# A recurrent-memory attention kernel: the order of loads, turns and value tails around its first segment

## The chip, the cores and the metric

The kernel runs on one core of a Trainium2 chip. The metric is device time in microseconds (us), the median of three runs; one further execution was profiled, and every line of a profile shown here is from such an execution. The engines are TensorE (PE, with its weight loads as PEld), VectorE (DVE), ScalarE (ACT), GpSimd (POOL) and SyncE (SP), which here does nothing but issue DMA transfers. DMA transfers are issued on SP's queue and on ACT's.

## What is computed

Two layers over 2048 tokens of width 640. The first is attention with a recurrent memory: the layer-normed tokens are cut into 64 segments of 32, each is put behind 8 memory rows, and the first 8 output rows of a segment are the memory of the next one. The second is a feed-forward layer with a squared ReLU. Cut to what matters:

```python
mem = mem0                                    # 8 x 640
for s in range(64):
    h = concatenate([mem, x[32 * s:32 * s + 32]])      # 40 x 640
    q, k, v = h @ Wq, h @ Wk, h @ Wv          # 32 heads of 128
    p = softmax(mask(q k^T * scale))          # memory columns open, the rest causal
    o = (p v) @ Wo                            # 40 x 640
    mem = o[:8]
    outs.append(o[8:])
h = x + concatenate(outs)
out = h + squared_relu(layernorm(h) @ w1 + b1) @ w2 + b2
```

The weights Wq, Wk, Wv and Wo are 5.24 MB each in bf16 and are kept on the core.

## The kernel before

**Segments, blocks and tails.** Four segments make a block of 128 tokens; there are 16 blocks (NB). One call of step(b, sp) (L459) works on segment sp of block b, and the recurrence makes the 64 steps a chain: the memory part of step s needs the output projection of step s - 1. A segment's 8 memory rows and first 24 tokens are the main rows, 32 in all, in tile hT4. The last 8 tokens of each segment, the tail, depend on no memory, so their q, k and v are projected a block at a time, away from the chain: load_tail_rows(g) (L144) loads the tails of four blocks (group g), ln_stats, ln_norm and ln_transpose (L184 to L229) turn them into hTt, and tail_units(b, which) (L312) gives ten pieces of work of four matmuls each, two halves of five. When a half is done, tail_out (L357) evacuates it on ACT: q and k are flipped into place by DVE, through the list late; v rows are stored to the DRAM tile vt_d and loaded back in another order by tails_v_in (L409) into vt4, one slot for each segment of the block.

**Row buffers and parking.** rowtile (L259) gives one of four buffers in turn for an evacuated row of 512. A value row goes instead into a place of the list parked, as long as there are any: memory that is used later for something else (hnT0, ht0, oTts, vt4s[1], hT4s[1], the v tile of step 1). It is then stored later, by the list stores, which the loop empties by 7, 5 and 5 at the starts of the steps (0, 1), (0, 2) and (0, 3). Before, there are 17 places, and block 0's rows don't use them: they are stored at once on ACT's queue.

**Fill.** The lists fill, late, mid, owed and soon hold work that steps take up at set places: run(q, n) does n pieces of q. What remains of fill is run at the end of a step, where PE would otherwise wait for the chain through mem_to_hT (L291).

**Before the first step.** Lines L155 to L160 and L825 to L837 issue the loads: x of block 0, the memory rows (four small loads on ACT's queue into a zeroed tile om, L156), tail group 0, Wv in five chunks, tail group 1, Wq, Wk, tail group 2, Wo in six pieces, x of block 1. All but the memory rows are on SP's queue. start() (L766) then projects segment 0 together with the tails of block 0 in three streams (v, q, k), chunk by chunk of the weights, into one PSUM tile pa; it puts tail units of later blocks between the chunks. Its result v0 makes step(0, 0) run with ready set: it has no projections of its own and takes fill in their place.

**Queues.** The order of the work is the program's (L109): each engine and each DMA queue does its instructions in the order in which the code issues them. PSUM has a pool mm of three buffers for single products and transposes, one buffer ch for scores and the output projection pw, and one of four banks for pa and po. wo_rounds (L273) does the output projection in 16 rounds; rounds 0 to 8 (the end left out, as in the calls) need the even heads of Wo, which are loaded first, rounds 8 to 12 the next two pieces, rounds 12 to 16 the last two.

Of the kernel before, what the change touches and what calls it, by code (L numbers as in the profile page):

```python
# [11 lines left out]
F32 = mybir.dt.float32  # L12
BF16 = mybir.dt.bfloat16
# [3 lines left out]
def kernel(  # L17
# [16 lines left out]
    nc = tc.nc  # L34
# [43 lines left out]
    ident = const.tile([128, 128], BF16)  # L78
    o_ring = [const.tile([64, DH], BF16, name="o%d" % k) for k in range(5)]
    o0 = const.tile([128, DC, 32], BF16, name="om")  # L80
    nc.vector.memset(o0[:], 0.0)
    make_identity(nc, ident[:])
# [47 lines left out]

    def load_w(w, src):
        w2d = src.rearrange("d h e -> d (h e)")
        for c in range(DC):
            nc.sync.dma_start(out=w[:, c * HE:(c + 1) * HE], in_=w2d[c * 128:(c + 1) * 128, :])
# [20 lines left out]
    load_x(0)  # L155
    for q in range(4):  # L156
        nc.scalar.dma_start(out=o0[32 * q:32 * q + M],  # L157
                            in_=A_mem0[0].rearrange("m (c q f) -> q m c f", q=4, f=32)[q])
    load_tail_rows(0)
    load_w(wv, A_Wv)  # L160

# [22 lines left out]
    def ln_stats(b):  # L184
        xns[b] = stats(xts[b][:])

    def ln_norm(b):
        mv, rs = xns[b]
        xn = s1.tile([128, D], BF16, tag="xn", name="xn")
        xt = xts.pop(b)  # L190
        nc.vector.tensor_scalar(out=xn[:], in0=xt[:], scalar1=mv[:, 0:1], scalar2=rs[:, 0:1],
                                op0=ALU.subtract, op1=ALU.mult)
        xns[b] = xn
# [56 lines left out]
    def mmtile():  # L250
        return mm.tile([128, 512], F32, tag="mm", name="ps")
# [52 lines left out]
    def run(q, n):  # L304
        while n > 0 and q:
            q.pop(0)()
            n -= 1
# [3 lines left out]

    def tail_units(b, which):  # L312
        w = {"q": wq, "k": wk, "v": wv}[which]
        lhs = lambda c: tail_rows(b, c)
        st = {}

        def unit(n, c):
            def f():
                if c == 0:
                    st[n] = mmtile()  # L320
                proj(w, "columns" if which != "v" else "order", lhs, n, st[n], c, c + 1)
                if c == DC - 1:
                    tail_out(b, which, n, st[n][:])
            return f
        return [unit(n, c) for n in range(2) for c in range(DC)]
# [31 lines left out]
    def tail_out(b, which, n, ps):  # L357
        kept = which == "v" and 0 < b and len(parked) > 0
        row = parked.pop(0) if kept else rowtile()[:]
        evac_row(which, row, ps)  # L360
        if which == "v":
            def store(eng=nc.sync):
                eng.dma_start(out=vt_d[b, 2 * n:2 * n + 2].rearrange("j r f -> r j f"),
                              in_=row.rearrange("r (j f) -> r j f", j=2))
            if kept:
                stores.append(store)
            else:
                store(nc.sync if b else nc.scalar)
            return
        if n == 0:  # L370
            tails.setdefault(b, {})[which] = s2.tile([128, H, 32], BF16, tag=which + "Tt", name=which + "Tt")
        dst = tails[b][which]
        late.append(lambda: flip(row, dst, n))
# [20 lines left out]
    def mem0_to_hT(hT4):  # L394
        mt = s1.tile([128, DC, 32], BF16, tag="pk", name="mt")
        nc.vector.transpose(out=mt[:], in_=o0[:])
        nc.vector.tensor_copy(out=hT4[:, :, 0, 0:M], in_=mt[:, :, 0:M])

# [6 lines left out]

    vt4s, stores = {}, []
    vt_d = dram.tile([NB, 4, 128, 2 * E], BF16)
# [51 lines left out]
    def step(b, sp, v=None):  # L459
# [5 lines left out]
        if not ready:  # L465
            v = vs.pop(0) if vs else s2.tile([128, EG], BF16, tag="v", name="v")
        run(late, 10 if b in (0, NB - 2, NB - 1) else 2)
        if sp == (1 if b else 3) and b + 1 < NB:
# [79 lines left out]
        run(owed[1], 2)  # L548
        run(late, 1)
        project("q", wq, qT, 1)  # L550
# [3 lines left out]
        elif not ready:  # L554
            spread(1)
        run(late, 10)
        run(owed[2], 1)
# [23 lines left out]
        if ready:  # L581
            run(fill, DC)
        if not ready:
# [20 lines left out]
        if not ready:  # L604
            proj(wv, "half", lhs, 1, ps1, 3, DC)
            nc.scalar.copy(out=v[:, 512:1024], in_=ps1[:])  # L606
        if not last and len(fill) > 7:
            run(fill, 1)
        if not last:
            pT1 = soft2(1)  # L610
        tk = s1.tile([128, HG, NK], F32, tag="tk", name="tk")
        nc.vector.tensor_tensor(out=tk[:], in0=skv, in1=mask[:].unsqueeze(1).to_broadcast([128, HG, NK]), op=ALU.add)
# [12 lines left out]
        wo_rounds(main, pw, 6, 8)  # L625
        run(fill, DC if ready else 1)
        wo_rounds(main, pw, 8, 12)
        if ready:
            run(fill, 2 * DC)
        wo_rounds(main, pw, 12, 16)  # L630
# [84 lines left out]
    for b in range(2):  # L715
        vt4s[b] = s2.tile([128, 4, 2, E], BF16, tag="vt4", name="vt4")
    parked += [vt4s[1][:, 2 * u:2 * u + 2].rearrange("p s u e -> p (s u e)") for u in range(2)]
    hnTs = [hnT0[:], ck(DC * NT).rearrange("p (c t) -> p c t", c=DC)]
# [47 lines left out]
    def start():  # L766

        v = s2.tile([128, EG], BF16, tag="v", name="v")
        vs.append(s2.tile([128, EG], BF16, tag="v", name="v"))
        hT4s[1] = s2.tile([128, DC, 4, SEG], BF16, tag="hT4", name="hT4")  # L770
        parked.append(hT4s[1][:, 0:4].rearrange("p c s t -> p (c s t)"))
        parked.extend(vs[0][:, 512 * u:512 * u + 512] for u in range(2))
        main = lambda c: hT4s[0][:, c, 0, :]
        units = []

        def stream(which, w, dst, k=0):
            pa = pop.tile([128, 4, 512], F32, tag="po", name="pa")
            for c in range(DC):
                for n in range(2):
                    proj(w, "half" if which == "v" else "columns", main, n, pa[:, n, :], c, c + 1)  # L780
                for n in range(2):
                    proj(w, "order" if which == "v" else "columns", lambda c: tail_rows(0, c), n, pa[:, 2 + n, :], c, c + 1)
                if c < DC - 1:
                    run(units, k)
            if which == "k":
                ln_stats(("t", 2))
            for n in range(2):
                if which == "v":
                    nc.scalar.copy(out=v[:, n * 512:(n + 1) * 512], in_=pa[:, n, :])
                else:  # L790
                    row = rowtile()[:]
                    evac_row(which, row, pa[:, n, :])
                    flip(row, dst, n)
                    tail_out(0, which, n, pa[:, 2 + n, :])
                    run(late, 100)
                    tails_in(0, 0, which, n * 16, (n + 1) * 16)
            if which == "v":
                for n in range(2):
                    tail_out(0, which, n, pa[:, 2 + n, :])

        stream("v", wv, None)
        ln_stats(("t", 1))
        ln_norm(("t", 1))
        units += tail_units(1, "v")
        run(units, DC)
        ln_transpose(("t", 1))()
        run(units, DC)
        units += tail_units(2, "v") + tail_units(3, "v") + tail_units(4, "v")
        stream("q", wq, qT, 7)
        for n in range(2):  # L810
            spread(n)
        units += tail_units(5, "v")
        run(units, 12)
        tails_v_in(0, nc.scalar, 0, 1)
        tails_v_in(0, nc.sync, 1, 4)
        units += tail_units(1, "q") + tail_units(6, "v")
        stream("k", wk, kT, DC)
        units += tail_units(1, "k")
        run(units, 2 * DC)
        run(late, 100)  # L820
        ln_norm(("t", 2))
        load_tail_rows(3)
        return v

    ln_stats(0)  # L825
    ln_norm(0)
    load_tail_rows(1)
    load_w(wq, A_Wq)
    ln_stats(("t", 0))
    ln_transpose(0)()  # L830
    mem0_to_hT(hT4s[0])
    ln_norm(("t", 0))
    load_w(wk, A_Wk)
    load_tail_rows(2)
    load_wo()
    load_x(1)
    ln_transpose(("t", 0))()  # L837
    v0 = start()
    halves = [h for b in range(7, 12) for h in (tail_units(b, "v")[:DC], tail_units(b, "v")[DC:])]
    halves.append(tail_units(12, "v")[:DC])  # L840
    quarters = [(b, "v", n, u) for b in range(12, NB) for n in range(2) for u in range(2)][2:]
    for b in range(NB):
        for sp in range(4):
# [3 lines left out]
            if b == 0:  # L847
                for h in range((6, 2, 2, 1)[sp]):
                    fill += halves.pop(0)
                if sp == 0:  # L850
                    fill.insert(2 * DC, lambda: ln_transpose(("t", 2))())
                if sp < 3:
# [162 lines left out]
```

## Time and profile before

| | us |
|---|---|
| median of three runs | 958.87 |
| lowest, highest | 958.25, 959.07 |
| the profiled execution | 958.06 |
| its span, first to last instruction | 956.3 |
| PE busy in the span | 929.1 (97%) |
| DVE busy | 699.7 (73%) |
| ACT busy | 548.4 (57%) |
| POOL busy | 258.2 (27%) |
| chain that ended last: PE, DMA, DVE, ACT | 93%, 3%, 2%, 1% |

The span is what lies between the first and the last instruction; the time adds what lies around it (1.8 us in the profiled execution). A window's row gives the busy time of each engine within it, with the number of instructions in brackets. A row of a timeline begins with start and length in us; a bracket at its end says how long the engine had been idle before and what ended that. A q behind an engine's name means its queue, that is the issuing of a DMA. Matmul ends are modelled: a following row can start before the one above it has ended, and the idle time in brackets is then shorter than the distance of the starts would give.

### The profile page before, as it was taken

Reading aid. Unit: us, or ns where it says so; the run is one execution under the profiler, and the core shown is the slowest. Engines: PE = TensorE matmul, PEld = TensorE weight load, DVE = VectorE, ACT = ScalarE, POOL = GpSimd, SP = SyncE. Lnnn points to the kernel's source line nnn. Section 1 sums busy time; section 2 is a strip of 40 time slices with the busy share of each in tenths; the row PEclk is TensorE's granted clock in tenths of the full one; section 3 lists DMA queues with packets and bytes.
Section 4 is the critical chain, followed back from the end, with each engine's and each line's share of the span. In section 5 each row is a group of like instructions: output and inputs, shape, how many; then the busy total and the mean of one; then the engine's idle time right before and its main releaser. Section 6 shows DMA issues by size and latency. Waiting matters only on the chain.

```text
span 956.3 us, 57547 instructions
## 1 busy us (share of the span) xinstructions
PE 929.1 (97%) x25874; PEld 570.3 (60%) x25883; DVE 699.7 (73%) x2136; ACT 548.4 (57%) x1343; POOL 258.2 (27%) x798
## 2 busy tenths in 40 slices
PE   4989999999999999999999999999999998999998
PEld 2545666666666666666666666656666665555555
DVE  3167778888888888888887787878787888566532
ACT  2556666666666666666666666656666665523321
POOL 1013222222222222222222222222222233263300
PEclk9999999999999999999999999999999999999999
DMA  9973210101010101010101010101010111643320
GB/s 360 396 235 90 45 29 13 29 13 30 10 33 9 34 10 34 9 34 9 33 10 34 9 32 11 32 11 32 11 32 11 53 43 21 199 113 86 94 56 28
DMA packets 60838, 56.74 MB, mean 59 GB/s; under 512 B 27696, under 2 KB 56752, under 8 KB 58672
## 3 DMA queue, kind: packets, MB, share of 16 engines
q1 hardware_dynamic: 59712, 52.73, 18.3%
q8 instruction: 202, 3.31, 1.5%
q10 hardware_dynamic: 880, 0.34, 0.1%
q14 instruction: 44, 0.36, 0.1%
HBM read 38.37 MB, written 9.44 MB: 50 GB/s over the span
## 4 chain that ended last, share of the span: by engine, by line
PE 93%; DMA 3%; DVE 2%; ACT 1%; issue 1%; ACTq 0%; DVEq 0%
PE ps L116 63%; PE pw L116 16%; PE y L116 6%; PE po L116 5%; DMA vt_d<-row 2%; PE sm L116 1%; PE pa L116 1%; DMA om<-in_A_mem_dram 1%; ACT otc L298 0%; ACTq L157 0%; ACT row L266 0%; DVE otr L297 0%; DVE kTt L269 0%; DVE qT L269 0%; DVE kT L269 0%
## 5 line engine op out<-in xcount | busy, mean ns | idle before, releaser
L116 PEld LDWEIGHTS <-hT 128*32 128x32 bf16 x8383 | 216.9, 96 | 146.2 <-DVE hT L300 20.7
L116 PE MATMUL pw<-wo,oT 128*32 128x320 bf16 x4224 | 178.4, 300 | 0.2
L116 PE MATMUL ps<-wv,hT 128*32 128x512 bf16 x2520 | 177.5, 380 | 0.0
L116 PE MATMUL ps<-wq,hT 128*32 128x512 bf16 (+1 forms) x3168 | 160.6, 336 | 4.8 <-DVE hT L300 4.8
L116 PE MATMUL ps<-wk,hT 128*32 128x512 bf16 (+1 forms) x2575 | 159.7, 375 | 0.0
L641 POOL TENSOR_TENSOR pkt<-ek,rk 128x64 bf16<-128x64 bf16 x64 | 19.3, 301 | 421.7 <-DVE rk L639 408.4
L116 PEld LDWEIGHTS <-oT 128*32 128x32 bf16 x4224 | 100.9, 96 | 44.8 <-ACT oT L257 9.1
L269 DVE STREAM_TRANSPOSE qT<-row 128x512 bf16<-128x512 bf16 x128 | 89.5, 699 | 24.4 <-ACT row L264 20.5
L264 ACT ACTIVATE row<-ps 128x512 bf16<-128x512 f32 (+1 forms) x170 | 93.7, 562 | 13.7 <-PE ps L116 11.7
L937 ACT ACTIVATE wv<-ps,b1f 128x512 bf16<-128x512 f32 (+1 forms) x56 | 37.6, 673 | 66.5 <-PE ps L116 66.0
L442 ACT CAST oT<-po 128x512 bf16<-128x512 f32 x128 | 74.7, 586 | 0.0
L298 ACT COPY otc<-otr 64x40 f32<-64x40 f32 x126 | 28.2, 224 | 71.5 <-DVE otr L297 71.1
L453 POOL COPY qz<-qT 128x96 bf16<-128x96 bf16 x126 | 33.5, 266 | 112.5 <-DVE mx L503 58.2
L116 PEld LDWEIGHTS <-hTt 128*32 128x32 bf16 x1640 | 45.1, 97 | 31.4 <-issue 2.0
L266 ACT CAST row<-ps 128x512 bf16<-128x512 f32 (+1 forms) x113 | 61.6, 560 | 1.9 <-PE ps L116 0.5
L635 DVE TENSOR_REDUCE zk<-ek 128x8 f32<-128x320 bf16 x64 | 31.1, 486 | 42.9 <-ACT ek L633 42.9
L116 PEld LDWEIGHTS <-v 32*128 32x128 bf16 x4064 | 42.1, 91 | 32.8 <-issue 18.4
L116 PE MATMUL y<-wq,wk 128*128 128x320 bf16 x448 | 61.2, 299 | 0.2 <-DVE wk L938 0.2
L484 ACT CAST row<-ps 128x256 bf16<-128x256 f32 x126 | 40.8, 376 | 30.3 <-PE ps L116 30.2
L257 ACT CAST oT<-po 128x128 bf16<-128x128 f32 x63 | 16.8, 267 | 65.3 <-PE po L116 65.3
L606 ACT CAST v<-ps 128x512 bf16<-128x512 f32 x63 | 37.0, 587 | 29.7 <-PE ps L116 29.7
L116 PEld LDWEIGHTS <-qz 128*32 128x32 bf16 x2016 | 36.0, 95 | 28.1 <-ACT em L506 1.9
(109 smaller groups left out, 1659.9 us busy)
## 6 DMA issues: line engine op xcount, KB each, us to landing
wv<-in_A_Wv_dram SPq DMA_DIRECT2D x5, 1024.0 KB
wq<-in_A_Wq_dram SPq DMA_DIRECT2D x5, 1024.0 KB
wk<-in_A_Wk_dram SPq DMA_DIRECT2D x5, 1024.0 KB
vt<-vt_d SPq DMA_DIRECT2D x60, 64.0 KB
xt<-in_A_x_dram SPq DMA_DIRECT2D x18, 160.0 KB
wo<-in_A_Wo_dram SPq DMA_DIRECT2D x2, 1280.0 KB
wo<-in_A_Wo_dram SPq DMA_DIRECT2D x4, 640.0 KB
wq<-in_B_w_dram SPq DMA_DIRECT2D x1, 2080.0 KB
```

The costliest lines, as they stand in the source:

```text
L116: nc.tensor.matmul(*a, **k)
L264: nc.scalar.mul(out=row, in_=ps, mul=scale)
L266: nc.scalar.copy(out=row, in_=ps)
L269: nc.vector.transpose(out=dst[:, n * 16:(n + 1) * 16, 0:32], in_=row.rearrange("p (h e) -> p h e", e=32))
L298: nc.scalar.copy(out=tc_[:, a], in_=tr[64:128, a, :, 0:M])
L442: nc.scalar.copy(out=oTg[:, n, :, :, M:NK], in_=po[:, :, n * 128:(n + 1) * 128].rearrange("p g (j q) -> p g j q", q=32))
L453: nc.gpsimd.tensor_copy(out=d.rearrange("p a (j f) -> p a j f", j=3)[:, :, :, 0:M], in_=src[:, :, 0:3, :])
L484: nc.scalar.copy(out=row[:, u * 256:(u + 1) * 256], in_=ps[:, u * 256:(u + 1) * 256])
L606: nc.scalar.copy(out=v[:, 512:1024], in_=ps1[:])
L635: nc.vector.tensor_reduce(out=zk[:], in_=ek[:], op=ALU.add, axis=AX.X)
L641: nc.gpsimd.tensor_tensor(out=pkt[:], in0=ek[:, :, SEG:NK], in1=rk[:].unsqueeze(2).to_broadcast([128, HG, TL]), op=ALU.mult)
L937: nc.scalar.activation(out=r[:, 0:w], in_=ps[:, 0:w], func=ACT.Relu, bias=b1f[:, fc:fc + 1], scale=1.0)
```

## The change

The memory rows are loaded by one transfer of eight whole rows on SP's queue, into a part of the tile ht0[3], and turned by five small PE transposes and one DVE copy in place of the DVE turn of a zeroed tile. Wv is loaded in two parts with tail group 1 between them; tail group 2 is loaded ahead of Wq. The norms of the tail groups are done earlier, and the turns of groups 1 and 2 stand in the streams v and behind stream q.

In start(), the value tails of blocks 1 and 2 are put between the chunks of the v stream, those of blocks 3 to 5 into the q stream, and those of blocks 6 to 8 into and ahead of the k stream, so that step (0, 0) has four halves as fill and the three steps behind it one each (before: 6, 2, 2, 1). Block 0's value rows take two parked places; one place is added (vrow), and one output buffer (o_ring) taken away. Of block 0's rows, slot 0 is stored at once on ACT's queue, and the whole rows later on SP's, behind Wo and x of block 1 and just ahead of the loads of slots 1 to 3. Step (0, 0) runs its late work behind the second softmax instead of at three places ahead of it, and its last fill behind the last Wo rounds.

```diff
-    o_ring = [const.tile([64, DH], BF16, name="o%d" % k) for k in range(5)]
-    o0 = const.tile([128, DC, 32], BF16, name="om")
-    nc.vector.memset(o0[:], 0.0)
+    o_ring = [const.tile([64, DH], BF16, name="o%d" % k) for k in range(4)]
...
     load_x(0)
-    for q in range(4):
-        nc.scalar.dma_start(out=o0[32 * q:32 * q + M],
-                            in_=A_mem0[0].rearrange("m (c q f) -> q m c f", q=4, f=32)[q])
+    mem0 = ht0[3][0:M, :]
+    nc.sync.dma_start(out=mem0, in_=A_mem0[0])
     load_tail_rows(0)
-    load_w(wv, A_Wv)
+    load_w(wv, A_Wv, 0, 2)
...
     def tail_out(b, which, n, ps):
-        kept = which == "v" and 0 < b and len(parked) > 0
+        kept = which == "v" and len(parked) > 0
...
+            if b == 0:
+                nc.scalar.dma_start(out=vt_d[b, 2 * n:2 * n + 2].rearrange("j (a s) f -> s a j f", s=4)[0],
+                                    in_=row.rearrange("(a s) (j f) -> s a j f", s=4, j=2)[0])
             if kept:
-                stores.append(store)
+                (stores if b else stores0).append(store)
             else:
-                store(nc.sync if b else nc.scalar)
+                store()
...
     def mem0_to_hT(hT4):
-        mt = s1.tile([128, DC, 32], BF16, tag="pk", name="mt")
-        nc.vector.transpose(out=mt[:], in_=o0[:])
-        nc.vector.tensor_copy(out=hT4[:, :, 0, 0:M], in_=mt[:, :, 0:M])
+        pt = mm.tile([128, 1024], BF16, tag="mm", name="pt")
+        for c in range(DC):
+            transpose(out=pt[:, c * M:(c + 1) * M], in_=mem0[:, c * 128:(c + 1) * 128], identity=ident[0:M, 0:M])
+        nc.vector.tensor_copy(out=hT4[:, :, 0, 0:M], in_=pt[:, 0:DC * M].rearrange("p (c m) -> p c m", m=M))
...
-        run(late, 10 if b in (0, NB - 2, NB - 1) else 2)
+        if not ready:
+            run(late, 10 if b in (0, NB - 2, NB - 1) else 2)
...
         if ready:
-            run(fill, DC)
+            run(fill, 5)
...
         if not last:
             pT1 = soft2(1)
+        if ready:
+            run(late, 100)
...
         wo_rounds(main, pw, 6, 8)
-        run(fill, DC if ready else 1)
+        run(fill, 4 if ready else 1)
         wo_rounds(main, pw, 8, 12)
-        if ready:
-            run(fill, 2 * DC)
         wo_rounds(main, pw, 12, 16)
...
+    parked.append(const.tile([128, 512], BF16, name="vrow")[:])
...
-        def stream(which, w, dst, k=0):
+        def stream(which, w, dst, ks):
...
-                if c < DC - 1:
-                    run(units, k)
-            if which == "k":
-                ln_stats(("t", 2))
+                if c < len(ks):
+                    run(units, ks[c])
+                    run(late, 100)
...
                     tail_out(0, which, n, pa[:, 2 + n, :])
-                    run(late, 100)
+                    late.pop()()
...
+        chtile = lambda: chn.tile([128, 512], F32, tag="ch", name="pc")
+        ahead = tail_units(1, "v")
+        late2 = tail_units(2, "v", (chtile, mmtile))
+        units += [u for c in range(DC) for u in (ahead[c], ahead[DC + c], late2[c])]
         ln_stats(("t", 1))
         ln_norm(("t", 1))
-        units += tail_units(1, "v")
-        run(units, DC)
-        ln_transpose(("t", 1))()
-        run(units, DC)
-        units += tail_units(2, "v") + tail_units(3, "v") + tail_units(4, "v")
-        stream("q", wq, qT, 7)
+        units.insert(9, lambda: ln_transpose(("t", 1))())
+        stream("v", wv, None, (3, 3, 4, 3, 3))
+        ln_stats(("t", 2))
+        ln_norm(("t", 2))
+        units += late2[DC:] + tail_units(3, "v") + tail_units(4, "v") + tail_units(5, "v")
+        run(units, 9)
+        stream("q", wq, qT, (7, 7, 7, 7))
         for n in range(2):
             spread(n)
-        units += tail_units(5, "v")
-        run(units, 12)
+        units.append(lambda: ln_transpose(("t", 2))())
+        units += tail_units(1, "q") + tail_units(6, "v") + tail_units(7, "v") + tail_units(8, "v")
+        run(units, 17)
         tails_v_in(0, nc.scalar, 0, 1)
+        run(stores0, 2)
         tails_v_in(0, nc.sync, 1, 4)
-        units += tail_units(1, "q") + tail_units(6, "v")
-        stream("k", wk, kT, DC)
+        stream("k", wk, kT, (6, 6, 6, 6))
         units += tail_units(1, "k")
-        run(units, 2 * DC)
-        run(late, 100)
-        ln_norm(("t", 2))
+        run(units, 100)
         load_tail_rows(3)
         return v
...
     load_tail_rows(1)
+    load_w(wv, A_Wv, 2)
+    ln_stats(("t", 0))
+    out0 = ln_transpose(0)
+    ln_norm(("t", 0))
+    out0()
+    mem0_to_hT(hT4s[0])
+    load_tail_rows(2)
     load_w(wq, A_Wq)
-    ln_stats(("t", 0))
-    ln_transpose(0)()
-    mem0_to_hT(hT4s[0])
-    ln_norm(("t", 0))
     load_w(wk, A_Wk)
-    load_tail_rows(2)
     load_wo()
...
-    halves = [h for b in range(7, 12) for h in (tail_units(b, "v")[:DC], tail_units(b, "v")[DC:])]
-    halves.append(tail_units(12, "v")[:DC])
+    halves = [h for b in range(9, 13) for h in (tail_units(b, "v")[:DC], tail_units(b, "v")[DC:])][:7]
...
-                for h in range((6, 2, 2, 1)[sp]):
+                for h in range((4, 1, 1, 1)[sp]):
                     fill += halves.pop(0)
-                if sp == 0:
-                    fill.insert(2 * DC, lambda: ln_transpose(("t", 2))())
```

## What was forecast

> **What bounds the kernel now.** The page first: TensorE (PE) is busy 929.1 us of a 956.3 us span and heads the chain with 93%, so a change to the opening can only win or lose PE idle time. Then the windows by ten microseconds, to see where that idle time lies (columns: window, length, then busy us of PE, PEld, DVE, ACT, POOL with instruction counts; granted clock; DMA share; GB/s):
>
> ```profile
> 0.00:10.00 10.00, 0.71 (x5) 0.45 (x5) 4.99 (x21) 1.84 (x2) 2.47 (x11) 1.00 0.77 286
> 10.00:20.00 10.00, 6.97 (x77) 2.75 (x81) 1.97 (x6) 1.60 (x2) 0.49 (x2) 1.00 1.02 411
> 20.00:30.00 10.00, 9.59 (x169) 4.73 (x165) 0.45 (x1) 5.72 (x10) 0.30 (x1) 1.00 1.01 418
> 30.00:40.00 10.00, 8.90 (x168) 4.81 (x161) 2.61 (x4) 5.39 (x10) 1.25 (x6) 1.00 1.02 420
> 40.00:50.00 10.00, 9.27 (x172) 5.03 (x165) 3.32 (x7) 4.85 (x9) 0.86 (x3) 1.00 1.05 352
> 50.00:60.00 10.00, 7.45 (x229) 4.36 (x232) 6.31 (x20) 5.21 (x12) 0.60 (x2) 1.00 1.00 341
> 60.00:70.00 10.00, 9.07 (x205) 4.63 (x201) 6.44 (x19) 5.82 (x14) 3.58 (x12) 1.00 0.44 128
> ```
>
> PE idles 18.0 us before 70 us, and from 70 to 100 us it is busy all the time. Just as important: the DMA engines are saturated from 10 to 60 us. Two resources, not one, bound the opening.
>
> The chain of waits over the first 75 us names the gaps:
>
> ```profile
> 3.75 8.19 DMA om<-in_A_mem_dram
> ...
> 13.74 6.92 PE pa L116 x70
> ...
> 23.34 14.29 DMA vt_d<-row
> ...
> 37.65 0.61 ACT row L264
> ...
> 64.27 4.50 PE ps L116 x75
> ```
>
> The memory rows land at 11.94 us and hold the first product until 13.7; block 0's value rows, stored through ACT's queue behind the weights, land at 37.6 and free a row buffer. The next two views show what that second one is, and the queue on which the change puts these rows:
>
> ```profile
> 37.65 0.60 ACT L264 ACTIVATE row<-pa 128x512 bf16<-128x512 f32 x1 [1.42 <-DMA vt_d<-row]
> ```
>
> ```profile
> 39.89 11.58 SPq L166 DMA_DIRECT2D wo<-in_A_Wo_dram x6
> 51.57 2.20 SPq L141 DMA_DIRECT2D xt<-in_A_x_dram  x1
> 53.81 2.77 SPq L416 DMA_DIRECT2D vt<-vt_d  x4
> ...
> 60.58 1.39 SPq L150 DMA_DIRECT2D ht<-in_A_x_dram  x2
> ...
> 65.36 0.37 SPq L363 DMA_DIRECT2D vt_d<-row  x1
> 65.78 1.01 SPq L363 DMA_DIRECT2D vt_d<-v  x2
> ```
>
> A full ring of four `row` buffers stops ACT until a store has landed. And SP issues strictly in program order: wo, x of block 1, four vt4 loads, four loads of tail rows (group 3), then value stores. The third L150 issue waited until 60.58 for a wo transfer: that dates wo's last landing to 60.6 (the landing events of the trace say 60.56).
>
> **The change, part by part.**
>
> *Front.* The four om loads, their 0.12 us memset and the DVE turn go; a whole-row load on SP takes their place, between x and the tail rows, which by the landing events were there at 3.0 and 4.3 us. Five small PE transposes and a DVE copy (0.17 us, as L397) follow at about 6.5 to 7.1 and 8.5, where PE had nothing from 6.51 to 13.03. What is late next is the norm of the tail rows: their POOL chain ends at 7.92, norm 0.45, five transposes 0.71 (13.03 row), first hTt copy 0.8 (half of 1.60). The v stream starts at 7.92+0.05+0.45+0.05+0.71 = about 9.1 instead of 13.67: **4.5 us**.
>
> *More work before step 0.* Blocks 7 and 8 (four halves of 1.08 us: 20 matmuls start at 39.15, the next group at 40.23) move from step 0 into the streams; parked block 0 removes the 1.10 us PE wait at 38.29; the q1 and k1 flips leave the chains before scores(0) and scores(1) (1.19 and 1.26 us on DVE, behind PE waits of 1.40 and 1.39). New PE waits appear: three tail evacuations (0.59 each) now stand on ACT before those of the v stream, and the turn of group 2 holds a PSUM buffer behind four q evacuations (2.1 us) plus its copies (1.59); I count 2.0 and 1.1 us. Then, with a stream at 4.3 us (80 matmuls at 0.054), a unit at 0.216 and a turn at 0.4: v stream 9.1 + 4.3 + 15 units 3.2 + turn 0.4 + 2.4 lost at the start's half speed (below) = 19.5; nine units and the 2.0 wait, 23.4; q stream with 26 units, 33.4; turn, 16 units, the 1.1 wait, 38.4; k stream with 24 units, 47.9; k1, 50.1; in step 0 14 units 3.0, scores and values 0.8, wo rounds 0 to 12 1.7 (48 matmuls), small waits 0.7: PE reaches the last wo rounds (12 to 16) at about 56.3, against 61.54.
>
> *wo comes no faster.* The same 21 MB pass the same saturated engines. Only ACT's block 0 stores shrink (512 packets of 27 ns to 128, over 16 engines: 0.65 us) and om's go (0.1). wo lands at 60.6 - 0.75 = **59.8** (59.0 to 60.6). In-order PE waits there 3.5 us; the fill that stood between rounds 8 to 12 and 12 to 16 is now behind them. Rounds 12 to 16 take 0.55 (61.54 to 62.09); from their end to the next step's first product another 1.34 passes (764.06 to 765.40 below, with a short fill). Step 1 starts at 59.8+0.55+1.3 = 61.7, against 64.27.
>
> *SP's queue.* Here I part from that gain. The block 0 stores (2 x 128 KB) are now issued on SP behind wo and x of block 1, and the loads of slots 1 to 3 read what they write, so SP stands until they land: 59.8 + 160 KB at about 350 GB/s (0.45) + 256 KB at 240 to 261 GB/s (the windows from 67 to 70, when only stores ran: 1.05) + 0.3 for the write's answer = 61.6. Queued behind that wait: four vt4 loads, 2.77 us of issue (53.81 row), four tail-row loads, 0.67 to 0.69 each with gaps (2.8 in all), and only then the stores of step 0's own value rows, at 67.2. A store landed about 1.8 us after issue (65.36 to 67.1, by its landing event): **69.1** (67.8 to 70.6, the ends of wo and of the 5.6 us of issue).
>
> The Trainium skill, "DMA: Bandwidth & Descriptors", section "Rules for kernel authors", says that a DMA reading what an earlier one wrote must wait for the first one's completion; sharing a queue does not order them. The trace agrees (SP's L416 waited 0.2 us for a `vt_d` store); if queue order sufficed, SP would not stand at 61.6 and the fourth case below would be the result.
>
> *The row ring.* With block 0 parked there are 18 parked places, and blocks 0 to 8 fill all. Step 0's four halves (blocks 9 and 10) therefore each take one of the four row buffers, and before, only one did (65.36 row). Counting on (q stream 4, q1 2, k stream 4, k1 2, then these 4), step 1's first q evacuation needs the buffer of block 9's first half: ACT waits from 62.8 to 69.1, as it did at 37.65. PE can still do three projections (three PSUM buffers), to 64.9, then idles 4.8 us. At 69.7 it starts k's second half (1.08); DVE's flips of q and k (0.65 each) end at 71.1, and scores(0) of step 1 comes at **71.1 against 68.59: 2.5 us late**. Afterwards v's buffers (stores issued from 69.3 to 70.3, landed by 72.1) are free when ACT writes v at about 72.6, so I add nothing.
>
> *What is given back.* Steps 1 and 2 each have one half less, 1.08. But four units then cover the memory chain at the end, as here:
>
> ```profile
> 764.06 1.04 PE L116 MATMUL ps<-wk,ht 128*32 128x512 bf16 x16
> 765.40 1.27 PE L116 MATMUL ps<-wq,hT 128*32 128x512 bf16 x36 [0.31 <-DVE hT L300]
> ```
>
> Sixteen matmuls at 0.054 end their issue at 764.92; 0.48 is lost. So each gives 0.60, together **1.2**. Step 3's fill is unchanged.
>
> *Costed at nothing.* Four o buffers instead of five: one write per 12 us step, and SP waits 422.9 us in all for these rows, so the store is long done; cover gone, it would be a store's 2 us once. Two 0.4 us ACT issues stay as they were. The wait of the group 2 load for the memory transposes (7.1) is hidden by 3 MB of wv still queued; without them SP would lose about 1 us.
>
> **Sum:** +2.5 - 1.2 = **+1.3 us**, on the profiled 958.06 (span 956.3 and 1.8 around it) 959.4. That execution lay 0.8 under the median of the three runs, so I forecast 958.87 + 1.3 = **960.2**. PE's 10 us of gained time all go into waits for wo and for a row buffer.
>
> One price is not in the trace: whether PE's clock halves over the 4.8 us idle. From below: the gaps of 0.9 to 1.4 us leave eight wide matmuls at 0.43 us (38.29 to 38.72, behind 1.10). From above: the first matmuls after 13.03 take 0.85 for eight until about 18.5, so 5 us at half speed cost 2.4, of which some 0.2 would hide behind the flips: 2.2. The row at 13.03 follows a longer gap (6.5) and an engine that had never run fast, so I take nothing and keep 2.2 as a case.
>
> **The rivals.**
>
> 1. *Clock falls* (slower): place, step 1 after the row wait; price 2.2; it decides if the idle stretch is long enough to throttle. +3.5, **962.4**. For it: matmuls at the start run at half rate. Against: the granted clock row reads full throughout, and no warm gap of this length exists before. The Trainium skill, "TensorE: Matmul & The Clock Gate", Part 1 (the HAM clock gate), puts the fall at about one idle window of 3.4 us, free-running; by that an idle 4.8 us is throttled in some cases only.
> 2. *No row wait* (SP passes, or stores land before 62.8): step 1 starts at 61.7, -2.6 - 1.2 = -3.8, **955.1**. For it: before, the wait on a row existed only on ACT's queue. Against: the count of buffers and SP's order.
> 3. *Nor a wo wait*: step 1 at 61.7 - 3.5 = 58.2, -7.3, **951.6**. Needs wo 3.5 us earlier from engines at a share of 1.0; hardly.
> 4. *The loads do not wait for the stores*: SP runs as before, no row wait, the same time as 2.
>
> **Chances.** Forecast 0.42, its own range 958.0 to 962.2 (69.1 between 67.8 and 70.6, rounded outward); clock 0.28; no row wait (2 and 4) 0.22; no wo wait 0.08. The range leaves out the last and the upper end of the clock case: **952.8 to 963.4**. A measurement here tells 0.2% (1.9 us) from no change. The forecast gives 0.28 of its 0.42 to "same" and 0.14 to slower, the clock case 0.24 to slower and 0.04 to same, the others 0.29 to faster and 0.01 to same: faster 0.29, same 0.33, slower 0.38.
>
> **What would show it.** Right: first `pa` matmul near 9 us; no ACT wait in the q stream; PE waiting on wo before the last `pw` rounds of step 0; SP silent from about 54 to 61.6, then L416, L150, L363 without a break; ACT's L264 in step 1 waiting several us for a `vt_d<-row` DMA. Matmuls of 0.85 per eight after 69 show the clock case. Wrong: step 1's first evacuation without a DMA wait, or wo landing before 57.

## The result and the profile after

On one chip the changed kernel took 962.09 us (median of 7 runs) and the kernel before 959.07: a ratio of 1.0029 with a 95% interval of 1.0016 to 1.0042, so slower by 3.0 us (1.5 to 4.0). The profiled execution took 962.09 with a span of 960.3, against 956.3 before. The forecast was 960.2, a loss of 1.3; 962.4 was the price of its first rival, the fallen clock. Two profiles of the experiments below, of `e1_warm` and `e5_change_again`, are of disturbed executions with a lower clock all through, so only the times of these two are compared.

First the windows of ten microseconds, in the columns used for the kernel before (the first figure after the instruction counts is the granted clock):

```profile
0.00:10.00 10.00, 2.38 (x23) 1.24 (x23) 5.47 (x22) 2.54 (x4) 2.47 (x11) 1.00 0.74 267
10.00:20.00 10.00, 8.05 (x125) 3.62 (x125) 1.54 (x4) 2.51 (x4) 0.79 (x2) 1.00 1.01 395
20.00:30.00 10.00, 7.86 (x120) 3.93 (x112) 1.54 (x4) 5.38 (x10) 0.79 (x2) 0.83 1.02 421
60.00:70.00 10.00, 6.01 (x117) 3.47 (x111) 3.88 (x12) 3.06 (x8) 1.59 (x4) 1.00 0.30 87
70.00:80.00 10.00, 9.94 (x288) 5.62 (x287) 7.93 (x27) 4.81 (x14) 1.97 (x8) 0.83 0.39 106
```

PE has 1.7 us more work in the first ten and 3.1 us less from 60 to 70. The granted clock is 0.83 in two windows where it read 1.00 before: the records give half speed for 3.41 us from 25.87 and again from 70.25. "Busy 9.94" in the last window is therefore not full speed: 288 matmuls were done in it, against 320 before.

The rows of PE's timeline at which it had waited longest, from the first product to step 1:

```profile
19.43 0.62 PE L114 MATMUL pa<-wv,hT 128*32 128x512 bf16 x8 [1.78 <-DMA wv<-in_A_Wv_dram]
25.21 0.62 PE L114 MATMUL pa<-wq,hT 128*32 128x512 bf16 x8 [2.14 <-ACT hnT L263]
40.65 1.48 PE L114 MATMUL ps<-wv,hTt 128*32 128x512 bf16 x24 [0.98 <-ACT hTt L218]
61.70 1.13 PE L114 MATMUL pw<-wo,oT 128*32 128x320 bf16 x27 [1.45 <-issue]
70.00 2.13 PE L114 MATMUL ps<-wk,hT 128*32 128x512 bf16 x20 [2.54 <-ACT row L261]
```

The second and third were forecast (2.0 and 1.1). The first and the fourth were not: the last chunk of wv landed at 19.4, and at 60 PE stood for something that no semaphore in the trace shows (the last section comes back to it). The fifth is the row wait, and its 20 matmuls take 2.13 where 20 of the same shape at full speed, at 80.13, take 1.26: the half clock.

The chain of waits of the same kernel, over the piece that decides, and behind it SP's queue and ACT's wait:

```profile
54.04 7.51 DMA vt_d<-hnT
61.56 0.02 SPq L417
...
67.37 1.90 DMA vt_d<-row
69.27 0.02 issue
...
69.35 0.61 ACT row L261
69.96 0.04 issue
70.00 2.11 PE ps L114 x18
```

```profile
53.22 1.41 SPq L360 DMA_DIRECT2D vt_d<-hnT  x2
61.61 2.72 SPq L417 DMA_DIRECT2D vt<-vt_d  x4
64.44 2.83 SPq L148 DMA_DIRECT2D ht<-in_A_x_dram  x4
67.37 2.00 SPq L360 DMA_DIRECT2D vt_d<-row  x4
```

```profile
69.35 0.60 ACT L261 ACTIVATE row<-ps 128x512 bf16<-128x512 f32 x1 [3.80 <-DMA vt_d<-row]
```

SP has issued block 0's two stores (`vt_d<-hnT`) by 54.6 and then stands until they have landed, at 61.56. It issues four vt4 loads and four tail loads and reaches the stores of step 0's rows at 67.37. One of these lands at 69.27, ACT, which has waited 3.80 us for its buffer, evacuates, and PE goes on at 70.0. Nothing of the opening is on this piece of the chain: it runs through DMA and SP's queue. Step 1 began at 64.00 (before 64.27) and step 2 at 80.13 (before 76.56): the opening won 0.27, step 1 lost 3.84. Step 2 took 11.75 instead of 12.30; from step 3 on the kernel is 3.0 behind, and scattered waits of later steps bring that to 4.0 at the end of this execution.

### The profile page after: what moved, and what is told of

Read it like the earlier page. It is cut to its first block, busy times and chain, and to the rows that moved or that the text cites. A ratio compares the mean times of both kernels' runs of the same rounds, so it can differ in the third digit from the quotient of the medians.

```text
span 960.3 us, 57580 instructions
## 1 busy us (share of the span) xinstructions
PE 933.5 (97%) x25883; PEld 587.5 (61%) x25883; DVE 702.3 (73%) x2134; ACT 547.4 (57%) x1343; POOL 257.1 (27%) x798
## 3 DMA queue, kind: packets, MB, share of 16 engines
q8 instruction: 202, 3.31, 1.5%
## 4 chain that ended last, share of the span: by engine, by line
PE 93%; DMA 2%; DVE 2%; ACT 2%; SPq 1%; issue 0%; ACTq 0%; DVEq 0%
PE ps L114 64%; PE pw L114 16%; PE y L114 6%; PE po L114 5%; PE sm L114 1%; DMA wv<-in_A_Wv_dram 1%; PE pa L114 1%; DMA vt_d<-hnT 1%; DVE wk L944 1%; DVE lnst L170 0%; ACT otc L295 0%; SPq L148 0%; ACT hnT L263 0%; SPq L417 0%; ACT row L261 0%
## 5 line engine op out<-in xcount | busy, mean ns | idle before, releaser
L114 PEld LDWEIGHTS <-hT 128*32 128x32 bf16 x8378 | 230.7, 96 | 139.1 <-DVE hT L297 21.1
L114 PE MATMUL ps<-wq,hT 128*32 128x256 bf16 (+1 forms) x3152 | 161.6, 337 | 4.3 <-DVE hT L297 4.3
L943 ACT ACTIVATE wv<-ps,b1f 128x512 bf16<-128x512 f32 (+1 forms) x56 | 37.5, 673 | 67.2 <-PE ps L114 67.0
L114 PE MATMUL y<-wq,wk 128*128 128x320 bf16 x448 | 61.6, 300 | 0.4 <-DVE wk L944 0.3
L266 DVE STREAM_TRANSPOSE kT<-row 128x512 bf16<-128x512 bf16 x65 | 45.7, 704 | 17.2 <-ACT row L263 14.9
```

Source lines behind the costliest of these rows:

```text
L114: nc.tensor.matmul(*a, **k)
L266: nc.vector.transpose(out=dst[:, n * 16:(n + 1) * 16, 0:32], in_=row.rearrange("p (h e) -> p h e", e=32))
L943: nc.scalar.activation(out=r[:, 0:w], in_=ps[:, 0:w], func=ACT.Relu, bias=b1f[:, fc:fc + 1], scale=1.0)
```

## The experiments

Twelve runs were made, in three groups of four, each group on one chip beside the kernel before (medians 957.71, 958.43 and 957.30). Times are medians in us; a ratio is to the kernel before on the same chip. The changed kernel itself, the control, is in the second and third group.

**PE kept at work in the row wait** (first try).

```diff
+        if b == 0 and sp == 1:
+            pd = pop.tile([128, 4, 512], F32, tag="po", name="pd")
+            for i in range(56):
+                r = slice(32 * (i % 4), 32 * (i % 4) + 32)
+                matmul(pd[r, i // 4 % 4, :], lhsT=tail_rows(0, 0), rhs=wv[:, 0:512], start=True, stop=True)
         project("k", wk, kT, 1, first_half)
```

> The changed kernel with 56 matmuls whose product nobody reads, put on PE in step 1 between the third projection and k's second half, where PE idles 2.7 us. Theory (row wait of 2.8 us, then half clock for 3.4 us): the row wait stays, ACT's q evacuation still waits until about 69.3 us, but the granted clock stays 1.00 from 70 to 74, k's second half takes 1.08 instead of 2.1 us, and step 2 starts 1.5 to 1.7 us earlier than in the changed kernel (80.13 there); time about 960.4. Rival (the clock is a bystander, the wait alone is the loss): clock fall gone, step 2 within 0.3 us of 80.13, time as the changed kernel's.

961.52, ratio 1.0034 (1.0021 to 1.0046): no gain over the 1.0029 of the first result. There was no control on this chip, so this settles nothing; two variants of it stand below, each beside a control.

**Tail group 3 loaded behind the value stores.**

```diff
         run(units, 100)
-        load_tail_rows(3)
...
                 if sp == 1:
-                    late.append(lambda: ln_stats(("t", 3)))
+                    load_tail_rows(3)
+                    mid.append(lambda: ln_stats(("t", 3)))
                     mid.append(lambda: ln_norm(("t", 3)))
```

> The changed kernel with the four loads of tail group 3 issued behind the value stores of step 1 instead of ahead of them; their statistics move to the end of step 1. Theory (step 0's stores are held up on SP's queue by what stands ahead of them): the first of these stores is issued 2.8 us earlier, at about 64.5, lands at about 66.4, ACT's wait for a row shrinks from 3.8 to about 1 us, PE's gap falls under 0.5 us, no half clock in step 1; step 2 starts at about 76.0 to 76.5 instead of 80.13; time about 958. Rival (the loss comes from the opening, late Wv and less fill): step 1 as long as before, 16 us, time within 0.5 us of the changed kernel's.

960.7, ratio 1.0035 (1.002 to 1.0049). Step 1 went the way of the theory, though not as far as it said: the row stores were issued at 65.04, ACT's row wait ended at 67.56 after 2.55 (expected: about 1), the clock stayed whole near 70, and step 2 began at 77.31, 2.8 earlier than in the changed kernel. But step 2 then took 13.60 instead of 11.75. Two rows of its timeline show why:

```profile
80.12 0.45 DVE L188 TENSOR_SCALAR xn<-ht,lnmv,lnrs 128x640 bf16<-128x640 bf16 x1 [1.64 <-POOL lnrs L175]
...
83.34 0.28 PE L114 MATMUL sm<-kT,qz 128*32 128x40 bf16 x16 [1.53 <-POOL qz L456]
```

The norm of the tail rows, now right behind its statistics, holds DVE 1.64 us for POOL; the flips of step 2's q and k stand behind it, and PE waits 1.53 for the scores' operand. So 1.85 of the 2.8 were given back by where this experiment put the norm. At step 3 it was still 1.0 ahead of the changed kernel's profile; the median shows nothing of that, and without a control on this chip it stays open where it went.

**Block 0's rows stored whole at once on ACT's queue.** The other parts of the change stay.

```diff
             if b == 0:
-                nc.scalar.dma_start(out=vt_d[b, 2 * n:2 * n + 2].rearrange("j (a s) f -> s a j f", s=4)[0],
-                                    in_=row.rearrange("(a s) (j f) -> s a j f", s=4, j=2)[0])
-            if kept:
-                (stores if b else stores0).append(store)
+                store(nc.scalar)
+            elif kept:
+                stores.append(store)
...
-        run(stores0, 2)
```

> The changed kernel with block 0's whole rows stored at once on ACT's queue, as before the change, from their parked places; nothing of block 0 is stored on SP. Theory: SP does not stop at 54 us, the loads of slots 1 to 3 are issued from 53 to 56 and step 0's value stores by about 60 as they are ready; no ACT wait for a row in step 1, no half clock there; step 2 at about 75.8 to 76.3; time 957.5 to 958.5. The weights may be 0.65 us later for 384 more small packets on ACT's queue. Rival (SP would be held up by wo and the tail loads anyway): ACT still waits over 2 us for a row in step 1 and the time stays above 960.

955.52, ratio 0.9983 (0.997 to 0.9996): faster than the kernel before, by 2 us more than expected. SP's queue and the row that ACT evacuates:

```profile
53.54 2.70 SPq L416 DMA_DIRECT2D vt<-vt_d  x4
56.94 5.07 SPq L148 DMA_DIRECT2D ht<-in_A_x_dram  x4
62.12 2.38 SPq L360 DMA_DIRECT2D vt_d<-row  x4
...
64.31 0.60 ACT L261 ACTIVATE row<-ps 128x512 bf16<-128x512 f32 x1 [0.22 <-DMA vt_d<-row]
```

The vt4 loads go at 53.54 instead of 61.61, the row stores 5.25 us earlier, and of the row wait 0.22 is left. Step 1 took 11.78 (16.13 in the changed kernel). So what this experiment undoes, block 0's rows stored late on SP's queue, cost the whole loss and more.

**The early start alone**, put into the kernel before: the memory rows in whole rows through small transposes, and with them the norm of tail group 0 ahead of the memory copy.

```diff
-    for q in range(4):
-        nc.scalar.dma_start(out=o0[32 * q:32 * q + M],
-                            in_=A_mem0[0].rearrange("m (c q f) -> q m c f", q=4, f=32)[q])
+    mem0 = ht0[3][0:M, :]
+    nc.sync.dma_start(out=mem0, in_=A_mem0[0])
```

> The kernel before with the front of the change alone: memory rows in whole rows on SP, turned by PE, norm of tail group 0 ahead of the memory copy; Wv in one part, everything else as before. Theory (wo's landing bounds step 0): PE starts its first product near 9.2 instead of 13.7 us, but step 1 starts only 0.5 to 1.5 us earlier (64.27 before), since wo lands at about 60; time 957.5 to 958.5 against 958.9. Rival (the start bounds the opening): step 1 starts 3 to 4.5 us earlier and the time is 954.5 to 956.

957.63, ratio 1.0002 (0.9993 to 1.001). The first product came at 9.09, 4.6 us earlier, and PE then waited for chunks of wv (0.78 and 1.60) and, later, of wk (0.81); half clock from 17.17 to 20.58 took more. Step 1 began 0.29 earlier, less than either expectation. The early start was worth nothing here, where the weights set the pace.

**The control on a second chip**: the changed kernel itself.

> The changed kernel itself once more, as the control for the three others on this chip. Theory: ratio to before 1.002 to 1.005, a row wait of 3.8 us on ACT at 69.3 and granted clock 0.50 for 3.4 us from about 70 in step 1. Rival (the half clock and its 1.1 us belong to one chip): full clock there, step 2 near 79 instead of 80.1.

960.71, ratio 1.0026 (1.0015 to 1.0036): the loss is there again, 2.3 us.

**The warm-up again**, the edit of the first try with 48 matmuls in place of 56.

> Adds 48 matmuls of 512 columns on 32 rows, whose product nobody reads, to PE's idle stretch in step 1 (some 2.7 us of work; 56 ended after the wait). Theory (idle time of PE halves the clock, and that costs step 1 its last 1.1 to 1.7 us): ACT's row wait stays at about 69.3, the granted clock is 1.00 from 70 to 74, k's second half takes 1.1 instead of 2.1 us, and the kernel is 1.0 to 1.7 us faster than the control. Rival (the half clock there is hidden by later waits): same as the control within 0.5 us, whatever the clock says.

961.17, 0.5 above the control: the time follows the rival, though the clock stayed whole. The chain of waits (start, length, what) shows where the lead was and where it went:

```profile
73.88 0.30 PE po L114 x20
74.18 0.55 PE ps L114 x8
74.72 0.87 PE pw L114 x24
75.59 0.53 PE po L114 x56
76.12 0.99 issue
77.11 0.19 PE po L114 x3
```

The products with the values come at 73.88, 1.1 us ahead of the changed kernel's 74.98, and at 76.12 PE stops for 0.99 with no semaphore behind it. The kernel counts PE's instructions in blocks of 256 and places the borders (its function align); 48 added matmuls are 96 instructions by that count and move the border. The trace bears this out: on the DMA queue for instructions a packet of 16 KB ended at 75.67, and PE went on 1.44 us behind it, the distance that all stops of this kind have (last section). The next warm-up, in the third group, adds fewer instructions.

**Tail group 3 loaded between the stores.**

```diff
-        load_tail_rows(3)
...
-                    soon.append(lambda n=(7, 5, 5)[sp]: [stores.pop()() for _ in range(min(len(stores), n))])
+                    soon.append(lambda n=(2, 5, 5)[sp]: [stores.pop()() for _ in range(min(len(stores), n))])
...
-                    late.append(lambda: ln_stats(("t", 3)))
-                    mid.append(lambda: ln_norm(("t", 3)))
+                    load_tail_rows(3)
+                    for _ in range(5):
+                        stores.pop()()
+                    mid.append(lambda: ln_stats(("t", 3)))
...
-                    ln_turn(("t", 3))
+                    late.append(lambda: (ln_norm(("t", 3)), ln_turn(("t", 3))))
```

> The four loads of tail group 3 stand on SP's queue behind step 0's four stores of rows and two of v and ahead of five other stores; their norm and turn are taken up where step 2 begins its late work. Theory (what stands ahead of the stores on SP's queue makes the row wait): stores of rows issued at about 65 instead of 67.4, ACT's row wait about 2.5 instead of 3.8, no half clock in step 1, step 2 starts at 76.9 to 77.3 instead of 80.1 and takes about 11.8; 2.5 to 3 us faster than the control, ratio to before 0.9995 to 1.001. Rival (the time comes back later, as when the norm stood at the end of step 1): same as the control within 0.5 us.

959.0, ratio 1.0006 (0.9996 to 1.0017), 1.7 faster than the control, between the two expectations. The stores were issued at 64.08, the row wait was 2.99, the clock stayed whole, step 2 began at 76.75, 3.4 earlier than in the changed kernel. Then it took 13.20: the norm again waited for POOL on DVE (1.29, at 79.56), and PE 1.14. So the queue order is worth some 3 us at the start of step 2, and a new wait took 1.5 of it.

**Wv in one part**, in the version with block 0's rows on ACT's queue.

```diff
-    load_w(wv, A_Wv, 0, 2)
+    load_w(wv, A_Wv)
...
-    load_w(wv, A_Wv, 2)
...
-        units.insert(9, lambda: ln_transpose(("t", 1))())
-        stream("v", wv, None, (3, 3, 4, 3, 3))
+        stream("v", wv, None, (3, 3, 3, 3, 3))
+        units += late2[DC:] + [lambda: ln_transpose(("t", 1))()] + tail_units(3, "v") + tail_units(4, "v") + tail_units(5, "v")
```

> The version that stores block 0's rows whole at once on ACT's queue, with Wv loaded in one part ahead of tail group 1, and the turn of group 1 behind the v stream. Theory (wo's last landing sets where step 1 starts, and the same bytes pass): wv's last chunk lands near 17.6 instead of 19.4, step 1 still starts at 62 to 63, 955.5 within 0.6 us, ratio to before 0.997 to 0.999. Rival (the opening's wait for wv, 1.8 us, and the half clock behind it set the start of step 1): 1.5 us or more faster than that, ratio under 0.997.

958.34, ratio 0.9998 (0.9988 to 1.0007), slower than that version's 0.9983. Neither expectation foresaw it. From the table of SP's waits up to 60 us, and PE's timeline:

```profile
SPq L132 <- DMA vt_d<-hnT: 13.2, 1, 13.2
```

```profile
58.50 0.32 PE L114 MATMUL pw<-wo,oT 128*32 128x320 bf16 x3 [0.80 <-DMA wo<-in_A_Wo_dram]
...
62.48 0.94 PE L114 MATMUL pw<-wo,oT 128*32 128x320 bf16 x14 [1.73 <-DMA wo<-in_A_Wo_dram]
```

A load of wk on SP waited 13.2 us for a value store of ACT's queue, whose semaphore it was given; the rate from 30 to 40 us was 372 GB/s (419 in the changed kernel), and PE waited for the last of wo until 62.48 (60.92 in the second profile of the version with Wv in two parts). The half clock came on top, from 62.85 to 66.26. Step 1 began at 65.51, against 62.54 and 62.80 with Wv in two parts, and took 12.22 where these took 11.78 and 11.92. So wo's landing does set the start of step 1 as soon as PE is there before it, which in the changed kernel's profile and in that of its control on the third chip it was not.

**Only SP's order altered**, on a third chip.

```diff
-        tails_v_in(0, nc.sync, 1, 4)
         stream("k", wk, kT, (6, 6, 6, 6))
...
-        load_tail_rows(3)
...
         run(fill, 4 if ready else 1)
+        if ready:
+            tails_v_in(0, nc.sync, 1, 4)
+            load_tail_rows(3)
```

> The changed kernel with only SP's order altered: the loads of slots 1 to 3 and the four loads of tail group 3 stand behind step 0's fill, so behind the stores of step 0's four value rows. Theory (SP standing for block 0's stores ahead of those row stores is the whole loss in step 1): the row stores are issued before 61, ACT's q evacuation in step 1 has no wait for a row, no half clock near 70, step 2 starts 11.8 to 12.1 us behind step 1, so at 74.4 to 76.1; 3.5 to 4.5 us faster than the control, ratio to before 0.998 to 0.9995. Rival (the later loads are missed in turn, or the time comes back in steps 2 and 3): faster than the control by under 1.5 us.

960.84, 1.1 below the control of this chip: the rival's number. But the edit did only half of what it was meant to, as SP's queue and ACT show:

```profile
56.20 2.05 SPq L360 DMA_DIRECT2D vt_d<-row  x2
61.98 2.75 SPq L417 DMA_DIRECT2D vt<-vt_d  x4
64.77 2.84 SPq L148 DMA_DIRECT2D ht<-in_A_x_dram  x4
67.71 0.93 SPq L360 DMA_DIRECT2D vt_d<-row  x2
...
69.69 0.60 ACT L261 ACTIVATE row<-ps 128x512 bf16<-128x512 f32 x1 [3.21 <-DMA vt_d<-row]
```

Two of the four row stores came ahead of the loads; the last halves of the fill ran later, and their stores stayed behind. Step 1's first two evacuations into a row went through. The third found no buffer until 69.69, and PE idled 3.76. So the wait follows the stores that stayed behind; all four ahead of the loads wasn't tried in this form.

**The warm-up with few instructions.**

```diff
-            align(s + b, 4 * 8 * DC + 32 + 1 + 16)
+            align(s + b, 4 * 8 * DC + 32 + 1 + 16 + 24 * (s == 1))
...
+        if s == 1:
+            pd = pop.tile([128, 4, 512], F32, tag="po", name="pd")
+            for i in range(12):
+                matmul(pd[:, i % 4, :], lhsT=ident[:], rhs=wv[:, 0:512], start=True, stop=True)
         project("k", wk, kT, 1, first_half)
```

> Adds 12 matmuls of 128 rows by 512 columns, whose product nobody reads, to PE's idle stretch in step 1 (about 2.6 us of work by 24 instructions; the run with 48 small ones had 96, and its lead of 1.1 us was lost in an issue wait of 0.99 at 76.1), and counts them in the placing of the instruction blocks. Theory (the half clock costs what it delays, and only the added instructions hid that): clock 1.00 from 70 to 74, no issue wait near 76, step 2 starts near 79, 1.0 to 1.7 us faster than the control. Rival (the price of the half clock is lost in other waits whatever is done): within 0.5 us of the control.

959.83, ratio 1.0029 (1.0018 to 1.0039), 2.1 below the control. PE's timeline in step 1:

```profile
67.08 2.54 PE L114 MATMUL pd<-wv,ident 128*128 128x512 bf16 x11 [0.16 <-issue]
70.15 1.26 PE L114 MATMUL ps<-wk,hT 128*32 128x512 bf16 x20 [0.54 <-ACT row L261]
...
79.35 1.26 PE L114 MATMUL ps<-wq,hT 128*32 128x512 bf16 x20 [0.30 <-DVE hT L297]
```

(The trace holds 11 of the 12 added matmuls in one row.) No half clock, no stop near 76. From k's second half to step 2 it is 9.20 us (70.15 to 79.35); in the control 10.26 (69.59 to 79.85), in the changed kernel's own profile 10.13. The half clock costs 1.06 us there; where the rest of the 2.1 comes from isn't shown. The two experiments on tail group 3, which kept a whole clock there too, took 9.10 and 9.11 us for the same stretch.

**Block 0's rows on ACT's queue, once more**, now beside a control.

> Once more the version that stores block 0's rows whole at once on ACT's queue, beside the control on one chip. Theory (no row wait): ratio to before 0.9975 to 0.999, 4 to 5 us faster than the control. Rival (its lead was that one chip's): 2 us or less faster than the control.

956.16, ratio 0.9986 (0.9974 to 0.9997), 5.8 below the control; step 1 took 11.92. Two chips agree: this version is faster than the kernel before, by 2.2 and 1.1 us in the medians, and by 5.8 than the changed kernel beside it.

**The control on the third chip.**

> The changed kernel itself, as the control for the three others on this chip: ratio to before 1.002 to 1.004, a row wait of 3.8 us in step 1 ending at 69.3, granted clock 0.50 for 3.4 us from about 70, step 2 at about 80.

961.93, ratio 1.005 (1.0036 to 1.0063), with a row wait of 3.95 to 68.95, half clock from 70.48, and step 2 at 79.85. In the three comparisons the change costs 2.3, 3.0 and 4.6 us.

## Where the prediction held and where not

*Front: right.* The first product came at 9.20 (forecast 9.1). *DMA as the second bound: right.* The early start alone gave 0.29 us at step 1.

*PE at the last wo rounds at 56.3: wrong, and with it the wait for wo.* PE began rounds 8 to 12 at 59.82 and rounds 12 to 16 at about 62.1. The last piece of wo had landed at 60.51 by its landing events (forecast 59.8; 60.56 before), so PE never waited for it. The 5.8 us can be read along the streams. The q stream began 1.8 late (25.21 for 23.4): my count of the v stream had no wait for its last chunk (1.78; tail group 1 stands inside Wv, and the rate of the first 20 us was lower by some 4 to 7%). The half speed at the start cost about 1.5 instead of 2.4 (the records show the full clock from 12.22), and terms that aren't broken down took that back. The q stream lost 1.7 more, with the half clock from 25.87. Step 0 lost 0.6, and the stop at 60 the remaining 1.7.

What the half clock at 25 us cost can be read from two experiments with the same opening that happened to keep a whole clock (the 48 matmuls, and tail group 3 between the stores). They came to the first wo rounds 1.5 to 1.8 earlier than the others (56.01 and 55.93, against 57.48 to 57.77) and began step 1 at 62.70 and 62.45, against 64.00, 63.45, 63.46, 63.46 and 63.47: about 1.0, the rest being lost in the stop near 60. Step 1 of the changed kernel began at 64.00, not 61.7. *It cost nothing*: the row store landed at 69.27, and ACT's evacuation came at 69.26 in the run that began step 1 1.3 us earlier. The later wait hides the opening, and PE's idle stretch was 2.54 instead of 4.8 for that reason.

*SP's queue and the row ring: right.* SP was free at 61.56 (61.6), the row stores were issued at 67.37 (67.2), one landed at 69.27 (69.1). That the first of these agrees so closely is in part luck: wo landed 0.7 later than forecast, and block 0's stores 1.05 behind it instead of 1.8, since their packets ran from 58 us on between those of wo. The 0.3 that I put down for the write's answer is shown by no run by itself. Rivals 2 to 4 fall with this step. The Trainium skill, "DMA: Bandwidth & Descriptors", section "Rules for kernel authors", which has a reading DMA wait for the completion of the writing one, agrees: SP's L417 waited 6.9 us for `vt_d<-hnT`. Where block 0's rows are stored early on ACT's queue, so that SP's loads find them there, row wait and loss are gone, on two chips.

*Clock at nothing: wrong.* I called the full clock likelier since gaps up to 1.4 had left it whole. Idle time of 2.54 was enough, with no need of the 4.8 forecast. The price, put at 2.2, is 0.93 in the changed kernel's profile and 1.06 in the control of the third chip, from k's second half to step 2 against the 9.20 of the run with 12 warm-up matmuls. Scores(0) came at 71.87 (forecast 71.1, before 68.59). Of the 0.93, 0.33 lies ahead of the scores (1.87 from k's second half to them, against 1.54 at full clock); in the control, where the clock fell later, all of the 1.06 lies behind them.

*Given back, 0.60 each in steps 1 and 2: right in step 2* (0.55); in step 1, which took 11.78 and 11.92 without a row wait against 12.29, it is 0.37 to 0.51.

The sum for the profiled execution: forecast +1.3, measured +3.0 at step 3. Of the 1.7 between, 0.93 is the half clock, the term put at nothing. 0.3 is k's second half starting at 70.0 for 69.7. Another 0.44 is the way from there to step 2, which takes 9.20 at full clock where the forecast comes to 8.76 (69.7 to 78.46, that is 76.56 + 2.5 - 0.6): the smaller give-back explains 0.1 to 0.2 of it, the rest isn't traced. Step 2 adds 0.05. So the measured 962.09 lands at the clock rival's 962.4 by about half of that rival's 2.2 and by smaller terms that it didn't have; that the two figures agree to 0.3 is luck.

## What to carry to other kernels

A queue that issues in order hands its wait to everything behind it: before a load that reads what a store has just written is put on a queue, list what stands behind it and who waits for that. Work won ahead of a resource that is late anyway (here the weights, then SP) is worth nothing; look first at what ends last. And a wait of two microseconds on PE can have a second price, in the matmuls that follow: whether it does hangs on how it falls into the stretches of the next section.

## What the runs showed of the hardware

- The half clock came in stretches of 3.41 us, after idle time far shorter than that. At single gaps: 2.54, 2.69 and 3.76 us in step 1, and one of 2.12 to 2.14 at 25 us in five profiles, but not in two others with the same gap. After 0.78 and 1.60 close together it came too, and after 0.36 and 1.73 (Wv in one part, 62.85); single gaps of 1.40 before the change and of 1.74, 1.81, 2.05 and 2.09 in the experiments left the clock whole. So the gap alone doesn't decide.
- The records show what does. Every full-speed stretch in them is a whole multiple of 3.41 us (13.65, 40.96 and 51.20 us are 4, 12 and 15 times that), as if the clock were set anew at a fixed beat. Cutting twelve of the profiles (all but those of `e1_warm` and `e5_change_again`) at that beat and adding up PE's idle time in each piece separates the cases: each of the ten falls in the first 110 us follows a piece with 1.95 to 2.54 us of idle time, and up to the end of the program none of the pieces that no fall follows has more than 1.95. In the two profiles that were spared at 25 us, the border cut the gap in two: the larger pieces held 1.41 and 1.95. That also tells why the half clock of step 1 began after work had resumed, by 0.25 us (70.00 and 70.25) to 1.2 us (71.77 and 72.97). The Trainium skill, "TensorE: Matmul & The Clock Gate", Part 1, puts a fall at about one idle window of 3.4 us, free-running: length and chance agree with the traces, the idle time that it takes does not, as 1.95 to 2.1 of the 3.41 us were enough.
- PE stood 0.4 to 1.66 us without a semaphore, most often at the wo rounds near 60 us (0.66 to 1.66 in every one of these profiles with the changed opening). The profile's DMA queues include one for instructions (202 packets, 3.31 MB, in the changed kernel). In the same twelve profiles, each of the 19 such stops of 0.3 us or more that lie before 860 us ended 1.36 to 1.61 us behind the end of a packet of 16 KB on that queue; the stop of the changed kernel ended at 61.70, the packet at 60.30. So PE stood for its own instructions, as far as times can show it. The packets near 60 us took 0.99 to 1.11 us, no longer than others between 35 and 82 us (0.89 to 1.69), so the full DMA engines did not slow them under way; whether they were asked for late no record shows.
